# Loading the first pair's keys in one transfer of 18 KB runs instead of two pieces

## The chip, the cores and the metric

The kernel runs on one core of a Trainium2 chip. The metric is device time in microseconds (us), as the median of several runs. A profile is one execution in which every instruction and every DMA packet was recorded; its span runs from the first to the last instruction and is 1.8 us shorter than the time that is reported for the same execution.

DMA packets carry a clock of their own, called the record clock here. It reads about 10.3 us more than the span's clock: the last packet of the fp32 weight strip ends at 14.59 on it, and the cast that waits for that strip starts at 4.29 us.

## The reference

Attention with keys and values averaged over groups of eight rows, followed by a soft mixture of experts with 32 slots. Shortened:

```python
# q, k, v: (8, 8, 576, 64) fp32; phi: (512, 32); w1: (8, 512, 1024); w2: (8, 1024, 512)
k_p = k.reshape(B, H, 72, 8, D).mean(axis=3);  v_p = the same of v
attn = softmax(q @ k_p.T / sqrt(D));  x = (attn @ v_p) laid out as (4608, 512)
logits = x @ phi
slot_input = softmax(logits, axis=0).T @ x                  # 32 slots, 4 per expert
slot_out[e] = relu(slot_input[e] @ w1[e]) @ w2[e]
out = softmax(logits, axis=1) @ slot_out                    # (4608, 512) fp32
```

## The kernel before

The batch is worked in four pairs. For each pair, q, k and v are loaded from fp32 in HBM to bf16 in SBUF by transfers that the Pool engine issues; these share one software queue with nearly all of the expert weights. A load into a buffer that is in use is issued only when its readers have finished. The parts that matter:

```python
big = ctx.enter_context(tc.tile_pool(name="big", bufs=4))       # q, k, v of a pair share four buffers

def load_pair(src, pair, name, cuts=()):
    t = big.tile([128, NT, D], BF, name=name, tag="big")        # NT = 72 rows of 64 per partition
    rows = src[2 * pair:2 * pair + 2].rearrange("b h (i t) d -> (b h i) t d", t=NT)
    for t0, t1 in zip((0,) + cuts, cuts + (NT,)):
        nc.gpsimd.dma_start(out=t[:, t0:t1], in_=rows[:, t0:t1])
    return t

nc.sync.dma_start(out=w1_f, in_=w1_rows[:, 0])                  # fp32 strip on another queue
k_sb[0] = load_pair(k, 0, "k_sb", cuts=(4 * POOL,))             # 32 rows, then 40 rows
q_sb[0] = load_pair(q, 0, "q_sb")
... # identity; cast of w1_f; then phi, v of pair 0, k of pair 1, q of pair 1, ...

def pool_stage(src, dst):                                       # averages groups of eight rows
    for r0 in range(0, NR, 4):                                  # NR = 9 groups: 0-3, 4-7, 8
        ... matmuls of src rows 8*r0 ... against pmat into pool_ps ...
        nc.scalar.copy(out=dst[:, r0:r0 + nr], in_=ps[:, 0:nr])

load_w2(E - 1, xpool, "xs", pieces=2)                           # the last load: two halves of the columns
...
for c in range(2):                                              # the end: per half of the columns
    second(E - 1, c)
    slots_out(c)
    for g in range(3):
        output(g, halves[c])
```

The softmax here doesn't subtract the row's maximum and nothing guards it: scores larger than these inputs give would overflow.

Of the kernel before, what the change touches and what calls it, by code (L numbers as in the profile page):

```python
# [18 lines left out]
def kernel(  # L19
# [10 lines left out]
    nc = tc.nc  # L30

    B, H, S, D = q.shape
    POOL = 8
# [11 lines left out]
    NT = S // NI  # L45
# [18 lines left out]
    pool_order = ctx.enter_context(ExitStack())  # L64
    pool_order.enter_context(tc.manual_schedule(engines={ET.Pool}))

    def load_pair(src, pair, name, cuts=()):
        t = big.tile([128, NT, D], BF, name=name, tag="big")
        rows = src[2 * pair:2 * pair + 2].rearrange("b h (i t) d -> (b h i) t d", t=NT)
        for t0, t1 in zip((0,) + cuts, cuts + (NT,)):  # L70
            nc.gpsimd.dma_start(out=t[:, t0:t1], in_=rows[:, t0:t1])
        return t

    w1_sb = persist.tile([128, E, DJ, F], BF)
# [13 lines left out]
    k_sb, q_sb, v_sb = [None] * NP, [None] * NP, [None] * NP  # L88
# [7 lines left out]

    hT = persist.tile([128, E, FJ, NS], BF)
    nc.vector.memset(hT, 0.0)
    k_sb[0] = load_pair(k, 0, "k_sb", cuts=(4 * POOL,))
    q_sb[0] = load_pair(q, 0, "q_sb")  # L100
    ident = consts.tile([128, 128], BF)
    make_identity(nc, ident)
    nc.gpsimd.tensor_copy(out=w1_sb[:, E - 1, 0], in_=w1_f)
    early.close()
    phi_f = persist.tile([128, DM // 128, NS], FP)
    nc.gpsimd.dma_start(out=phi_f, in_=moe_phi.rearrange("(p j) e -> p j e", j=DM // 128))
    v_sb[0] = load_pair(v, 0, "v_sb")


# [33 lines left out]
    for r in range(2):  # L143
        rows = slice(r * D, (r + 1) * D)
        nc.vector.tensor_copy(out=iphi[rows, :, 0:D],
                              in_=ident[rows, rows].rearrange("p d -> p () d").to_broadcast([D, H, D]))
# [301 lines left out]
    for n in [2] * NSMALL + [4] * ((NO - NSMALL) // 2):  # L448
        row0 = sum(128 * g[1] for g in groups)
        step_ = n // 2  # L450
        rows = lambda r, c0=row0 // 2, s=step_: cT[:, r % 2, c0 + r // 2:c0 + 128 * s:s]
# [88 lines left out]
```

## Time and profile before

| | |
|---|---|
| time | 179.69 us, median of 3 runs, 178.59 to 180.0 |
| span of the profiled execution | 175.9 us |
| software queue | 30.74 MB written, 6144 packets |
| first key product | 10.65 us |
| q of pair 0: first transpose | 17.89 us |
| last weights used by PE, first and second half of the columns | 147.19 and 149.82 us |

From the page of the kernel before, in 40 equal slices of 4.4 us: the clock granted to TensorE, the busy share of the DMA engines (9 is 90% or more) and the rate. Below them, for two DMA queues, packets, MB and share of the 16 engines.

```profile
PEclk9998589999999999999997598589965579999555
DMA  5999999999999999999999999999999999799995
GB/s 162 195 215 222 214 217 216 220 212 218 211 218 217 220 212 215 213 219 216 212 218 216 218 209 216 216 218 218 212 214 220 214 191 131 254 401 417 417 419 237
...
q0 software_dynamic: 6144, 30.74, 85.6%
...
q8 instruction: 11, 0.18, 0.4%
```

The DMA engines are busy without a gap and move about 216 GB/s up to slice 32. The stores take the last slices at about 417 GB/s.

The timeline of the kernel before, for the first pair's keys and q (start, duration, engine, line, operation, count; in brackets the idle time before it and what ended it):

```profile
1.25 1.23 POOL L71 DMA_DIRECT2D k_sb<-in_k_dram  x2 [0.81 <-POOLq L524]
...
10.65 1.06 PE L192 MATMUL pool_ps<-pmat,k_sb 128*128 128x128 bf16 x16
...
12.44 1.29 PE L192 MATMUL pool_ps<-pmat,k_sb 128*128 128x128 bf16 x20 [0.73 <-DMA k_sb<-in_k_dram]
...
14.03 0.53 POOL L71 DMA_DIRECT2D q_sb<-in_q_dram  x1 [7.06 <-PE pool_ps L192]
...
17.89 1.46 PE L207 MATMUL q_ps<-ident,q_sb 128*128 128x128 bf16 x12 [4.16 <-DMA q_sb<-in_q_dram]
```

PE pools the first piece while the second is on its way, then waits more than 4 us for q. The early start buys nothing that the next step can use.

The last part of the timeline of the kernel before: the matmuls of the last expert, for the two halves of the columns, and the first store.

```profile
147.19 0.40 PE L475 MATMUL so_ps_2188<-w_xs,hT 128*32 128x256 bf16 x8 [0.18 <-DMA w_xs<-in_moe_w_dram]
149.21 0.60 SPq L494 DMA_DIRECT2D out_dram<-o_sb_2328  x1
149.82 0.40 PE L475 MATMUL so_ps_2189<-w_xs,hT 128*32 128x256 bf16 x8 [0.28 <-DMA w_xs<-in_moe_w_dram]
```

The chain of waits of the kernel before has this as its longest piece (start, duration):

```profile
118.59 28.55 DMA w_xs<-in_moe_w_dram
```

The last weights are issued at 118.6 us and are waited for until 147.2 us: they sit behind everything else in the queue.

### The profile page before, as it was taken

How to read it: one execution, taken by the hardware profiler on the slowest of the kernel's cores; microseconds unless marked ns; L12 is line 12 of the kernel's file. 1: busy time of each engine (PE TensorE's matmuls, PEld its weight loads, DVE VectorE, ACT ScalarE, POOL GpSimd, SP SyncE). 2: the span in 40 equal slices, each digit the busy share in tenths (PEclk: the TensorE clock that was granted, in tenths of full speed). 3: DMA queues.
4: the chain of work that ended last, by engine and by line, in shares of the span. 5: the costliest groups of instructions: out<-in, count | busy, mean ns of one | idle time of the engine just before them, and what ended most of it. 6: DMA issues, size and time to landing. Idle time of an engine off the chain costs nothing.

```text
span 175.9 us, 3513 instructions
## 1 busy us (share of the span) xinstructions
PE 135.8 (77%) x1467; PEld 85.0 (48%) x1467; DVE 91.6 (52%) x251; ACT 79.3 (45%) x144; POOL 19.1 (11%) x38
## 2 busy tenths in 40 slices
PE   4981789899999999999998995998762277674700
PEld 1450657666876587865775453644651123221200
DVE  6200651378767868878688369643600003784530
ACT  3011158788958669676698540111100001684420
POOL 5501011102110601111001111003000000000000
PEclk9998589999999999999997598589965579999555
DMA  5999999999999999999999999999999999799995
GB/s 162 195 215 222 214 217 216 220 212 218 211 218 217 220 212 215 213 219 216 212 218 216 218 209 216 216 218 218 212 214 220 214 191 131 254 401 417 417 419 237
DMA packets 9086, 40.91 MB, mean 233 GB/s; under 512 B 736, under 2 KB 4320, under 8 KB 4976
## 3 DMA queue, kind: packets, MB, share of 16 engines
q0 software_dynamic: 6144, 30.74, 85.6%
q1 hardware_dynamic: 2928, 9.96, 14.3%
q8 instruction: 11, 0.18, 0.4%
q14 instruction: 3, 0.02, 0.0%
HBM read 61.93 MB, written 9.44 MB: 406 GB/s over the span
## 4 chain that ended last, share of the span: by engine, by line
DMA 43%; PE 36%; DVE 8%; ACT 7%; issue 1%; POOL 1%; DVEq 0%; SPq 0%; ACTq 0%
DMA w_xs<-in_moe_w_dram 16%; DMA q_sb<-in_q_dram 10%; DMA phi_f<-in_moe_phi_dram 7%; PE sc L265 6%; PE pool_ps L192 6%; PE G_ps L296 6%; PE u_ps L278 6%; PE q_ps L207 4%; DMA out_dram<-o_sb_2435 3%; DMA out_dram<-o_sb_2393 3%; DVE xs L284 2%; DMA w_f<-in_moe_w_dram 2%; PE lg_ps L290 2%; DMA out_dram<-o_sb_2336 1%; PE fold_ps L218 1%; ACT ex_1641 L266 1%
## 5 line engine op out<-in xcount | busy, mean ns | idle before, releaser
L284 DVE TENSOR_TENSOR xs<-u_ps,rec 128x384 bf16<-128x384 f32 x72 | 39.4, 552 | 1.6
L265 PE MATMUL sc<-qT,kp 64*72 64x288 bf16 x128 | 23.1, 311 | 0.6 <-ACT ex_1642 L266 0.4
L283 DVE RECIPROCAL rec<-u_ps 128x4 f32<-128x4 f32 x72 | 12.5, 175 | 16.8 <-PE u_ps L278 16.4
L207 PE MATMUL q_ps<-ident,q_sb 128*128 128x128 bf16 x144 | 13.1, 243 | 6.1 <-DMA q_sb<-in_q_dram 4.5
L488 PE MATMUL f_ps<-so,cT 128*128 128x512 bf16 (+1 forms) x42 | 12.0, 390 | 7.0 <-ACT o_sb_2435 L490 1.4
L207 PEld LDWEIGHTS <-q_sb 128*128 128x128 bf16 x144 | 10.0, 109 | 7.9 <-DMA q_sb<-in_q_dram 5.9
L265 PEld LDWEIGHTS <-kp 64*72 64x72 bf16 x128 | 8.7, 108 | 7.8 <-issue 2.0
L296 PE MATMUL G_ps<-xs,ee 128*128 128x512 bf16 x36 | 11.3, 454 | 0.4 <-ACT ee L291 0.4
L490 ACT ACTIVATE o_sb_2328<-f_ps,recR 128x256 f32<-128x256 f32 x1 | 0.5, 473 | 24.5 <-PE f_ps L488 24.5
L211 ACT COPY qT<-q_ps 128x768 bf16<-128x768 bf16 x8 | 6.4, 796 | 11.2 <-PE q_ps L207 11.2
L213 DVE COPY qT<-q_ps 128x768 bf16<-128x768 bf16 x16 | 8.8, 551 | 4.8 <-PE q_ps L207 4.7
L488 PEld LDWEIGHTS <-cT 128*128 128x128 bf16 x42 | 4.3, 103 | 14.2 <-issue 11.8
L195 ACT CAST kpar<-pool_ps 128x512 bf16<-128x512 f32 (+1 forms) x12 | 5.5, 484 | 11.4 <-PE pool_ps L192 11.3
L479 DVE TENSOR_SCALAR so<-so_ps_2188,recC 128x256 bf16<-128x256 f32 x1 | 0.5, 483 | 19.3 <-PE so_ps_2188 L475 19.3
L192 PE MATMUL pool_ps<-pmat,k_sb 128*128 128x128 bf16 x144 | 9.9, 220 | 0.8 <-DMA k_sb<-in_k_dram 0.7
L115 PEld LDWEIGHTS <-zeros 128*128 128x128 bf16 x53 | 5.6, 113 | 10.1 <-issue 4.5
L475 PEld LDWEIGHTS <-hT 128*32 128x32 bf16 x128 | 4.0, 109 | 11.8 <-issue 11.4
L192 PE MATMUL pool_ps<-pmat,v_sb 128*128 128x128 bf16 x144 | 9.6, 220 | 0.0
L192 PEld LDWEIGHTS <-k_sb 128*128 128x128 bf16 x144 | 8.5, 97 | 1.7 <-DMA k_sb<-in_k_dram 0.9
L192 PEld LDWEIGHTS <-v_sb 128*128 128x128 bf16 x144 | 8.2, 98 | 0.7 <-issue 0.2
L238 DVE TENSOR_TENSOR spread<-phi_f,head 128x256 bf16<-128x256 f32 x4 | 1.4, 422 | 12.4 <-DMA phi_f<-in_moe_phi_dram 12.4
L115 PE MATMUL warm_ps<-zeros 128*128 128x512 bf16 x18 | 6.0, 507 | 2.3 <-DVE ones L134 2.3
(171 smaller groups left out, 246.4 us busy)
## 6 DMA issues: line engine op xcount, KB each, us to landing
w_sb<-in_moe_w_dram POOLq DMA_DIRECT2D x7, 1024.0 KB, 31.8
q_sb<-in_q_dram POOLq DMA_DIRECT2D x4, 1152.0 KB, 18.9
v_sb<-in_v_dram POOLq DMA_DIRECT2D x4, 1152.0 KB, 17.1
w_big<-in_moe_w_dram POOLq DMA_DIRECT2D x4, 1024.0 KB, 37.2
k_sb<-in_k_dram POOLq DMA_DIRECT2D x3, 1152.0 KB, 21.6
w_qT<-in_moe_w_dram POOLq DMA_DIRECT2D x2, 1024.0 KB, 36.0
w_xs<-in_moe_w_dram POOLq DMA_DIRECT2D x1, 1024.0 KB, 37.2
w_xs<-in_moe_w_dram POOLq DMA_DIRECT2D x2, 512.0 KB, 29.4
```

What stands on the lines that cost most here:

```text
L115: nc.tensor.matmul(out=ps, lhsT=zeros[:, 0:128], rhs=zeros, start=True, stop=True)
L192: nc.tensor.matmul(out=ps[:, r].rearrange("p n i -> p (n i)"), lhsT=src[:, tt:tt + 2, :].rearrange("p t d -> p (t d)"), rhs=pmat, start=(t ...
L195: nc.scalar.copy(out=dst[:, r0:r0 + nr], in_=ps[:, 0:nr])
L207: nc.tensor.transpose(out=ps[:, t].rearrange("p n i -> p (n i)"), in_=q_sb[pair][:, tt:tt + 2, :].rearrange("p t d -> p (t d)"), identity= ...
L211: nc.scalar.copy(out=dst, in_=ps)
L213: nc.vector.tensor_copy(out=dst, in_=ps)
L265: nc.tensor.matmul(out=ps[:, r, 0:S // 2], lhsT=kp[pair][rows, n], rhs=qT[pair][rows, n], start=True, stop=True)
L278: nc.tensor.matmul(out=ps[rows, hh], lhsT=ex[b][:, hh].rearrange("p r t -> p (r t)")[:, c:c + rows.stop - rows.start], rhs=vp[(2 * pair + ...
L283: nc.vector.reciprocal(out=rec, in_=ps[:, :, XW])
L284: nc.vector.tensor_tensor(out=xs[pair][:, t, qd * HQ:(qd + 1) * HQ, :], in0=ps[:, :, 0:XW], in1=rec.rearrange("p h -> p h ()").to_broadcas ...
L296: nc.tensor.matmul(out=ps, lhsT=ee[:, t].rearrange("p g s -> p (g s)"), rhs=x[:, t, :, 0:D], start=(t == 0), stop=(t == 8))
L488: nc.tensor.matmul(out=f_ps, lhsT=rows(r), rhs=so[:, cols], start=True, stop=True)
```

## The change

The split let PE start on the first 32 rows of keys while the other 40 were still coming. The change drops it: one issue instead of two, and source runs of 18 KB per partition instead of 8 and 10 KB.

```diff
-    def load_pair(src, pair, name, cuts=()):
+    def load_pair(src, pair, name):
         t = big.tile([128, NT, D], BF, name=name, tag="big")
-        rows = src[2 * pair:2 * pair + 2].rearrange("b h (i t) d -> (b h i) t d", t=NT)
-        for t0, t1 in zip((0,) + cuts, cuts + (NT,)):
-            nc.gpsimd.dma_start(out=t[:, t0:t1], in_=rows[:, t0:t1])
+        nc.gpsimd.dma_start(out=t, in_=src[2 * pair:2 * pair + 2].rearrange("b h (i t) d -> (b h i) t d", t=NT))
         return t
 ...
-    k_sb[0] = load_pair(k, 0, "k_sb", cuts=(4 * POOL,))
+    k_sb[0] = load_pair(k, 0, "k_sb")
```

## The prediction

> **What bounds the kernel now.** Until 147 us it is the cast-loading software DMA queue. The forty-slice page shows the DMA engines at 9 tenths in every slice from 4.4 us on; a table of stretches gives a steady 216 GB/s from 24 to 140 us. The chain of waits ends its first part with the last expert weights (issued 118.6 us, landed 147.2 us, 28.6 us of queueing), then come about 23 us of output stores. Loads are issued long before they land: the list of DMA issues has 17 to 22 us for q, k, v and 32 to 37 us for weights. So what happens before 147 us counts only if it changes the queue's start, its work or leaves it empty.
>
> **What the change does.** Pool issues one key transfer (4608 elements per partition) instead of two (2048 and 2560). No instruction moves on PE, DVE, ACT or SP.
>
> 1. *Queue work, a small gain.* The trace's records of single packets give medians of 324 ns for 4096 bytes, 399 for 5120, 625 for 8192 and 700 for 9216. Both pieces cost 723 ns per partition, the whole 700: 23 ns saved. With 128 partitions over 16 engines that is 8 x 23 = 0.18 us, plus one 22 ns completion record: 0.2 us of queue time.
>
> 2. *Issue time, no gain.* Two key issues take 1.23 us on Pool, one about 0.55 to 0.7. The q issue moves from 2.46 to about 1.9 us, but q queues behind the keys anyway, and phi's issue (5.35 us) still waits for the fp32 weight strip, which lands at 4.24 us.
>
> 3. *Pooling starts later, no loss.* Now PE pools the first 16 products from 10.4 to 11.8 us, waits 0.7 us for the second piece and ends near 13.8 us. Afterwards it waits for the whole transfer (landing about 12.2 us), then does 36 products at about 62 ns, ending near 14.6 us. The next work, the q transposes, waits for q until 17.9 us in any case; the fold that reads kpar is at 23.2 us. The refill of the keys' buffer (pair 1's q) goes from 14.0 to about 14.9 us, but v of pair 0 and k of pair 1 (2.3 MB, over 8 us) are queued then, so the queue doesn't run dry.
>
> 4. *Possible side effect.* PE's idle gap before the q transposes shrinks from 4.1 to about 3.2 us. In this trace the clock drops to 0.57 in 18 to 24 us, and those transposes take 120 ns instead of 60. The Trainium skill, "TensorE: Matmul & The Clock Gate", Part 1, says that the clock halves after an idle window of about 3.4 us; the trace agrees so far. The clock may stay up, and pair 0's scores start 1 us sooner. That too is absorbed by the queue.
>
> **On the critical path:** only item 1, 0.2 us of 179.7, about 0.1%. The three runs before spread over 1.4 us.
>
> **Prediction:** 179.5 us, 178.0 to 181.0 us; faster by over 2%: 1%, within 2%: 97%, slower by over 2%: 2%.
>
> **Right if** the page shows 128 fewer software packets; the last weights land at 147.0 +/- 0.5 us; the first key product is at about 12.3 us instead of 10.4; q's first transpose stays at 17.5 to 18 us; DMA stays at 9 in all slices after the first.
> **Wrong if** the first transfer starts or lands much later as one piece (q's transposes then shift by as much, and so does the end), if an idle DMA slice shows a refill that came too late, or if the output stage differs (clock, stores).

## The result, and the profile after

The changed kernel took 179.99 us (179.67 to 180.23, 6 runs) against 179.50 us of the kernel before (178.59 to 180.0, 6 runs). The ratio is 1.0031, with a 95% interval of 1.0005 to 1.0058. A ratio is the mean time of one kernel's runs over that of the other's in the same rounds, so it isn't quite the ratio of the medians.

The interval excludes 1, and the changed kernel's profile is 2.3 us longer than that of the kernel before: 178.2 us against 175.9 us. (The profiled execution of the kernel before took 177.69 us, less than any of its six timed runs.) Taken alone, these two results would say that the one transfer costs something. From the page of the changed kernel:

```profile
PEclk9999657999999999999999975699975569569985
DMA  5999999999999999999999999999999997799995
GB/s 151 165 203 217 221 213 217 217 215 217 215 217 214 217 215 217 216 211 219 217 210 221 213 214 218 213 215 219 215 213 219 210 193 96 239 379 425 425 416 235
...
q0 software_dynamic: 6000, 30.74, 84.7%
```

There are 144 packets fewer: 128 data packets and the 16 four-byte completion records of one transfer. The first slices move less: 151 and 165 GB/s against 162 and 195. The timeline of the changed kernel for the first pair:

```profile
1.25 0.69 POOL L69 DMA_DIRECT2D k_sb<-in_k_dram  x1 [0.80 <-POOLq L522]
...
12.30 2.18 PE L190 MATMUL pool_ps<-pmat,k_sb 128*128 128x128 bf16 x36 [1.88 <-DMA k_sb<-in_k_dram]
...
14.78 0.53 POOL L69 DMA_DIRECT2D q_sb<-in_q_dram  x1 [8.11 <-PE pool_ps L190]
17.80 0.84 PE L205 MATMUL q_ps<-ident,q_sb 128*128 128x128 bf16 x12 [3.32 <-DMA q_sb<-in_q_dram]
```

Pooling now waits for the whole transfer, ends 0.75 us later, and is still idle for 3.3 us before q, which is there at the same time as before (17.80 and 17.89 us). So nothing is lost up to here. Yet the end of the loads has moved. The same part of the timeline of the changed kernel, and the longest piece of its chain of waits:

```profile
149.15 0.40 PE L473 MATMUL so_ps_2187<-w_xs,hT 128*32 128x256 bf16 x8 [0.19 <-DMA w_xs<-in_moe_w_dram]
151.17 0.60 SPq L492 DMA_DIRECT2D out_dram<-o_sb_2327  x1
151.77 0.40 PE L473 MATMUL so_ps_2188<-w_xs,hT 128*32 128x256 bf16 x8 [0.27 <-DMA w_xs<-in_moe_w_dram]
```

```profile
118.28 33.45 DMA w_xs<-in_moe_w_dram
```

The last weights are used 1.95 us later, although q is used 0.1 us sooner. The time was lost somewhere between 18 and 149 us, where the two programs are the same. That is the question for the experiments.

### The profile page after: what moved, and what is told of

Read it like the earlier page. It is cut to its first block, busy times and chain, and to the rows that moved or that the text cites. A ratio compares the mean times of both kernels' runs of the same rounds, so it can differ in the third digit from the quotient of the medians.

```text
span 178.2 us, 3512 instructions
## 1 busy us (share of the span) xinstructions
PE 136.2 (76%) x1467; PEld 85.5 (48%) x1467; DVE 92.0 (52%) x251; ACT 79.5 (45%) x144; POOL 18.4 (10%) x37
## 4 chain that ended last, share of the span: by engine, by line
PE 44%; DMA 33%; ACT 9%; DVE 6%; issue 1%; POOL 1%; DVEq 0%; ACTq 0%; SPq 0%
DMA w_xs<-in_moe_w_dram 19%; PE pool_ps L190 9%; PE sc L263 8%; DMA phi_f<-in_moe_phi_dram 7%; PE u_ps L276 7%; PE q_ps L205 5%; PE G_ps L294 5%; DMA out_dram<-o_sb_2434 3%; DMA out_dram<-o_sb_2392 2%; PE fold_ps L216 2%; DVE xs L282 2%; PE f_ps L486 2%; DMA w_f<-in_moe_w_dram 2%; PE lg_ps L288 2%; ACT ex_1640 L264 1%; ACT ex_1641 L264 1%
## 5 line engine op out<-in xcount | busy, mean ns | idle before, releaser
L486 PE MATMUL f_ps<-so,cT 128*128 128x512 bf16 (+1 forms) x42 | 12.9, 422 | 5.9 <-ACT o_sb_2462 L488 1.4
L205 PE MATMUL q_ps<-ident,q_sb 128*128 128x128 bf16 x144 | 12.6, 234 | 4.7 <-DMA q_sb<-in_q_dram 3.3
L205 PEld LDWEIGHTS <-q_sb 128*128 128x128 bf16 x144 | 9.5, 104 | 6.3 <-DMA q_sb<-in_q_dram 3.5
L190 PE MATMUL pool_ps<-pmat,v_sb 128*128 128x128 bf16 x144 | 10.8, 235 | 0.0
L294 PE MATMUL G_ps<-xs,ee 128*128 128x512 bf16 x36 | 9.8, 407 | 0.4 <-ACT ee L289 0.4
L190 PEld LDWEIGHTS <-v_sb 128*128 128x128 bf16 x144 | 9.5, 107 | 0.8 <-issue 0.2
L193 ACT CAST vpar<-pool_ps 128x512 bf16<-128x512 f32 (+1 forms) x12 | 5.6, 480 | 5.5 <-PE pool_ps L190 5.4
```

The source lines that it names most:

```text
L190: nc.tensor.matmul(out=ps[:, r].rearrange("p n i -> p (n i)"), lhsT=src[:, tt:tt + 2, :].rearrange("p t d -> p (t d)"), rhs=pmat, start=(t ...
L205: nc.tensor.transpose(out=ps[:, t].rearrange("p n i -> p (n i)"), in_=q_sb[pair][:, tt:tt + 2, :].rearrange("p t d -> p (t d)"), identity= ...
L294: nc.tensor.matmul(out=ps, lhsT=ee[:, t].rearrange("p g s -> p (g s)"), rhs=x[:, t, :, 0:D], start=(t == 0), stop=(t == 8))
L486: nc.tensor.matmul(out=f_ps, lhsT=rows(r), rhs=so[:, cols], start=True, stop=True)
```

## The experiments

Six theories were on the table in the end:

- **A**: the large first packets make the queue start slowly. In the first two profiles the slow key packets (those that took over 1.1 times the usual time of their size) were 19 engine-us over that time in sum in the changed kernel, against 8 in the kernel before.
- **B**: chance in the start of the queue.
- **C**: PE pools later, refills a buffer later, or runs on a colder clock, and that costs the time.
- **D**: the number of transfers decides, not the packet size.
- **E**: writing the descriptors of the next loads slows the large packets in flight.
- **F**: the start doesn't differ where it counts; something else on the DMA engines delays the slowest of them.

### The kernel before again, and the changed kernel again

No edit; both are yardsticks.

> The kernel before again, unchanged, as a yardstick for noise. Ratio 1.000 within 0.003 under every theory. The start of the queue: theory A (the whole key transfer starts the queue slowly, and does so every time) expects its packets to look like the first trace of before: 4096 and 5120 byte packets, in sum about 8 engine-us above their usual 324 and 399 ns in the first 20 us, first 2 MB landed some 1 us sooner than in the changed kernel. Theory B (the two traces differ by chance of the start) expects this sum to wander between 8 and 18.

Measured: 178.98 us, ratio 0.9977 (0.9919 to 1.0034); span of its profile 175.8 us.

> The changed kernel again. A: 0.3 to 0.6% slower than before (0.5 to 1.1 us), packets of the keys again slow (sum near 18 engine-us over 700 ns each), last expert weights landing again 1 to 2 us after those of the repeated kernel before. B: ratio 1.000 within 0.002, packets anywhere. C (later pooling, later refill or a cold PE clock costs the time): same ratio as A, but explained by the PE side, so the run with both pieces and late pooling must show it too.

Measured: 179.47 us, ratio 0.9988 (0.9923 to 1.0053). The 0.3% of the first result did not come back, though the interval is too wide to exclude it. The scatter was much larger: both kernels ran from about 177.2 to 180.5 us. The profile is 178.4 us long; this one execution counts as slow by the rule of 1.5% over the kernel's own fastest run. The sum of slow packets was 4.6 engine-us for the kernel before and 18.9 for the changed kernel, so A still stood in the packets, though not in the times.

### Two pieces, but late pooling

```diff
-        for r0 in range(0, NR, 4):
+        for r0 in (8, 4, 0) if late_first else range(0, NR, 4):   # late_first for pair 0's keys
```

> Two pieces as before, but pair 0's pooling takes the second piece's rows first, so PE starts when both have landed, as in the changed kernel (first key product at about 12.3 us instead of 10.4, refill at about 14.9 us). A: ratio 1.000, the queue starts as before. C: ratio 1.003 to 1.006, as in the changed kernel. B: 1.000.

Measured: 178.83 us, ratio 1.0008 (0.9956 to 1.0059). The timeline of this run shows that the edit did what it should: all 36 products in one block at 12.09 us and the refill at 14.57 us, as in the changed kernel.

```profile
12.09 2.18 PE L192 MATMUL pool_ps<-pmat,k_sb 128*128 128x128 bf16 x36 [0.40 <-DMA k_sb<-in_k_dram]
...
14.57 0.53 POOL L71 DMA_DIRECT2D q_sb<-in_q_dram  x1 [7.73 <-PE pool_ps L192]
17.58 0.95 PE L207 MATMUL q_ps<-ident,q_sb 128*128 128x128 bf16 x12 [3.30 <-DMA q_sb<-in_q_dram]
```

Its span is 176.0 us. In this profile the late pooling costs nothing, and the times show no cost either (to within half a per cent), which speaks against C.

### Two pieces, the first one small

```diff
-    k_sb[0] = load_pair(k, 0, "k_sb", cuts=(4 * POOL,))
+    k_sb[0] = load_pair(k, 0, "k_sb", cuts=(POOL,))
```

> Two pieces, cut at 8 rows instead of 32: packets of 1024 and then 8192 bytes. A in the form 'large packets are slow while the queue starts': 8192 byte packets above their 625 ns as in the changed kernel, and most of its loss, ratio 1.003 to 1.005. A in the form 'only the first few packets count, a short first transfer starts faster': ratio 1.000. B and C: 1.000 (C: PE waits 1 us longer than before for its second group, so at most 1.002).

Measured: 179.38 us, ratio 1.0018 (0.9968 to 1.0068), slow packets 13.1 engine-us. It lies between the two kernels and tells nothing apart.

### The changed kernel a third time, halves of the partitions, earlier issues, four pieces

> The changed kernel a third time, for its profile and the yardstick of this chip. Two earlier profiles of it landed 1.2 MB of the software queue's bytes at 21.8 and 22.0 us of the record clock (kernel before and the late-pooling run: 20.2 to 20.7) and ended the queue at 162.1 and 162.4 (before: 159.8 to 160.2). Theory A (the large packets of the first transfer are slow while the queue starts, every time): again 21.5 to 22.2 and 161.5 to 162.6. Timed: between 1.000 and 1.006; the last session's scatter of 3 us hides less than 0.5%.

Measured: 179.28 us, ratio 1.0022 (0.9986 to 1.0059); span 176.7 us. 1.2 MB were in at 20.9 and the queue ended at 160.7, so both expected ranges of A were missed.

Halves of the partitions, whole rows:

```diff
+        if pair == 0 and name == "k_sb":
+            rows = src[0:2].rearrange("b h (i t) d -> (b h i) t d", t=NT)
+            for p0 in (0, 64):
+                nc.gpsimd.dma_start(out=t[p0:p0 + 64], in_=rows[p0:p0 + 64])
+            return t
```

> The keys in two transfers again, but by halves of the partitions: whole rows, 9216 byte packets as in the changed kernel, and two issues as in the kernel before. If packet size makes the slow start (A): 1.2 MB at 21.5 to 22.2, end of the queue 161.5 or later. If the number of transfers or issues does (D): as the kernel before, 20.2 to 20.7 and 159.7 to 160.3.

Measured: 179.55 us, ratio 1.0032 (0.9996 to 1.0069). 1.2 MB were in at 20.6, as D expects, but the queue ended at 160.6, outside D's range.

Earlier issues, in the changed kernel:

```diff
+    nc.gpsimd.dma_start(out=phi_f, ...)          # moved up, from behind the cast of w1_f
+    v_sb[0] = load_pair(v, 0, "v_sb")
+    k_sb[1] = load_pair(k, 1, "k_sb")
     ident = consts.tile([128, 128], BF)
     make_identity(nc, ident)
```

> The changed kernel with phi, v of pair 0 and k of pair 1 issued straight after q (at 2.5 to 4.1 us instead of 5.0 to 6.7). In the two profiles of the changed kernel the slow packets start 5 to 7 us into the span, the same time as those issues. Theory E (writing descriptors for them slows the large packets in flight): the slow packets move to 2.5 to 4.1 us or vanish. A without E: they stay at 5 to 7 us, 1.2 MB again at 21.5 to 22.2.

Measured: 179.53 us, ratio 1.0009 (0.9961 to 1.0058). The slow packets fell to 9.0 engine-us but neither vanished nor moved to 2.5 to 4.1 us (they start from 3.1 to 9.1 us), which speaks against E. 1.2 MB were in at 20.7, and yet the queue ended at 162.3.

Four pieces:

```diff
-    k_sb[0] = load_pair(k, 0, "k_sb", cuts=(4 * POOL,))
+    k_sb[0] = load_pair(k, 0, "k_sb", cuts=(2 * POOL, 4 * POOL, 6 * POOL))
```

> Keys in four pieces (2048, 2048, 2048 and 3072 byte packets), the kernel before taken further. A: no slow start, packets within 10% of their usual time, 1.2 MB at 20.0 to 20.7; the extra packets cost 16 x 24 ns = 0.4 us of queue time against two pieces, so the end of the queue 159.8 to 160.6; ratio 1.000 to 1.003. If the gain goes on with ever smaller pieces: end before 159.6.

Measured: 179.52 us, ratio 1.0035 (1.0003 to 1.0068). The packets of 2048 bytes, whose usual time is 173 ns, were slow too: 16.4 engine-us in sum, almost as much as in the changed kernel. 1.2 MB were in only at 21.5, and the queue ended at 162.0. A had expected otherwise in all three.

After eight runs the measures disagreed with each other: a good start went with a late end, and packets of 2 KB were as slow as packets of 9 KB. The measure was at fault. "1.2 MB landed" is a mean over sixteen DMA engines. The Trainium skill, "DMA: Bandwidth & Descriptors", section "Why a DMA increments its semaphore by 16 and not by 1", says that the engines of a transfer finish independently and that only the full count means that all of the data has landed. The packet records agree: each transfer of this queue ends with 16 four-byte completion records, and the first and the last of them lie 1.4 to 4.9 us apart (from pair 0's v on). What PE waits for is the last of the sixteen.

### Following the slowest engine

So the sixteen completion records of each transfer were sorted, and the last was kept. For the kernel before, the intervals between these last completions repeat the same few numbers (worked out from the packet records). They start at the landing of pair 0's q, taken here together with phi, the 64 KB transfer behind it, which lands at most about 0.2 us later:

```
kernel before        5.47 5.47 5.47 5.47 5.47 5.47 5.47 4.87 5.47 5.47 5.47 4.87 (6x) 3.66 4.87 (6x) 4.66 2.66 2.87
changed kernel       5.47 6.40 5.47 5.47 5.47 5.47 5.47 4.87 5.47 5.47 5.47 4.87 (4x) 5.05 4.87 3.66 4.87 5.79 4.87 (4x) 3.75 2.76 3.66
```

A pair's load takes 5.47 us on an engine, an expert's weights take 4.87 us. The changed kernel has three intervals that are longer, by 0.93, 0.18 and 0.92 us, together 2.03 us. In the record clock, the first runs from 33.7 to 40.1, the second from 108.2 to 113.2 and the third from 126.6 to 132.4; instruction fetches of 16 KB started at 34.9, 110.9 and 127.0. The record of such a fetch is 0.89 to 0.98 us long. The idea is that the engine that serves it falls behind by about that much, and that the landing moves only if this engine is the slowest one or nearly so.

All sixteen completions, followed from one transfer to the next in the same records, show it. (The records do not name the engine; the one completion of sixteen that leaves the common step is taken for one engine.) In the first profile of the kernel before, each of the ten fetches from 34.8 to 138.9 delays one completion, by 0.85 to 1.11 us, and each time one that was 1.3 to 2.9 us ahead of the last, so that the last does not move. In the first profile of the changed kernel, three of the ten fetches delay completions that were only 0.18, 0.93 and 0.19 us ahead of the last, by 1.11, 1.12 and 1.11 us. What is left over, 0.93, 0.19 and 0.92 us, is the three stretches.

All profiles of kernels with an unchanged end, in the record clock; "q landed" includes phi, as above; "lost" is the end of the queue minus this landing minus 131.81 us, which is that difference in the first two profiles of the kernel before:

| kernel | keys landed | q landed | end of the queue | lost after q | span |
|---|---|---|---|---|---|
| before, first profile | 22.76 | 28.39 | 160.19 | 0 | 175.9 |
| before, again | 22.32 | 27.95 | 159.75 | 0 | 175.8 |
| late pooling | 22.17 | 27.80 | 159.92 | 0.31 | 176.0 |
| before, once more (below) | 22.73 | 28.36 | 162.25 | 2.08 | 178.3 |
| changed, first profile | 22.58 | 28.21 | 162.06 | 2.04 | 178.2 |
| changed, again | 22.62 | 28.25 | 162.40 | 2.34 | 178.4 |
| changed, third | 22.22 | 27.85 | 160.67 | 1.01 | 176.7 |
| changed, fourth (below) | 22.46 | 28.09 | 162.15 | 2.25 | 178.2 |
| small first piece | 22.19 | 27.82 | 161.17 | 1.53 | 177.2 |
| halves of the partitions | 21.04 | 26.66 | 160.57 | 2.10 | 176.8 |
| halves, again (below) | 22.31 | 27.96 | 161.74 | 1.97 | 177.7 |
| earlier issues | 22.62 | 28.25 | 162.29 | 2.23 | 178.2 |
| four pieces | 22.34 | 27.97 | 162.04 | 2.26 | 178.5 |

Among the first 24 intervals of these thirteen profiles, 27 are off their usual length by over 0.1 us. In 24 of the 27 a 16 KB fetch started. Fetches fall into 10 of the 24 intervals of any profile, so chance would give about 11 of 27. Two of the other three are one record counted into the neighbouring interval (-0.41 and +0.41). In the third, the 0.32 us of the late-pooling run, a smaller fetch started: 8 KB on queue q14, 0.32 us long. The span follows the end of the queue with an offset of 15.7 to 16.5 us in all thirteen.

The start of the queue does matter in one way. When pair 0's v landed, 1 or 2 engines (the slowest included) were within 1 us of the slowest one in the three profiles that lost least (0 to 0.31 us), and 3 to 10 engines in nine of the ten others (earlier issues: 2). So the more engines start late, the more of them are exposed to a fetch that counts.

This theory, F, was found after the fact, and needed a test on new runs.

### The test of F on new runs

> The kernel before once more. In ten profiles so far the last record of the software queue comes 131.8 us after the slowest DMA engine has finished pair 0's q, plus what that engine lost to 16 KB instruction fetches (0 to 2 of them, each about 0.9 to 1.1 us, seen as a stretched interval between two of its completions where 5.47 or 4.87 us is usual). Theory F (the start is the same, and fetches that hit the slowest engine make the difference): keys' landing at 22.2 to 22.8 of the record clock, end = q's landing + 131.8 + the stretches, to 0.1 us. Theory A (the whole key transfer starts the queue late): this one's keys land sooner than those of the changed kernel in the same call.

Measured: 179.79 us, ratio 0.9968 (0.9933 to 1.0003). This is the kernel before, unchanged, and its profile has a span of 178.3 us, 2.4 us longer than its first. It had lost 2.08 us after q, in stretches of 0.96, 0.14 and 0.97 us, which sum to 2.07; fetches started in all three of these intervals. (That landing plus stretches gives the end is arithmetic; what is tested is where the keys land and whether fetches start in the stretched intervals.) Its slow packets sum to 18.0 engine-us, as many as in the changed kernel. Its end, in the timeline:

```profile
149.37 0.40 PE L475 MATMUL so_ps<-w_xs,hT 128*32 128x256 bf16 x8 [0.18 <-DMA w_xs<-in_moe_w_dram]
...
151.39 1.94 SPq L494 DMA_DIRECT2D out_dram<-o_sb  x3
152.02 0.40 PE L475 MATMUL so_ps<-w_xs,hT 128*32 128x256 bf16 x8 [0.30 <-DMA w_xs<-in_moe_w_dram]
```

Read next to the first profiles, this is the end of the changed kernel (149.15 and 151.77), in a kernel that has the two pieces. Its first slices are as thin as those of the changed kernel too:

```profile
GB/s 153 156 219 224 211 223 209 225 207 221 211 221 211 224 209 219 214 215 215 217 215 215 215 214 218 213 215 219 213 215 217 212 192 82 226 392 423 423 419 235
```

So neither the late end nor the thin start needs the one transfer. A, which ties them to it, falls with this run; that the start varies from one execution to the next, as B has it, stands.

> The changed kernel once more. F: keys' landing on the slowest engine 22.2 to 22.8 as in the kernel before, end = q's landing + 131.8 + the stretches, to 0.1 us; timed ratio 1.000 within 0.004. A: keys and q land 0.5 us or more later than in the repeated kernel before, and the end too, without stretches.

Measured: 179.45 us, ratio 0.9962 (0.9928 to 0.9996), which leans the other way than the first result. Keys and q landed at 22.46 and 28.09, within F's range and not 0.5 us later than in the run above. It lost 2.25 us: 0.53, 0.59 and 0.53 us in intervals with fetches, and 0.58 us in the last three transfers, which were not followed engine by engine. With the fetches' stretches alone, F's "to 0.1 us" is missed by this 0.58 us.

> The keys by halves of the partitions once more. Its one profile landed the keys at 21.0 and q at 26.7, some 1.4 us before every other kernel, and lost 2.1 us of it again to two stretched intervals. If that start is a property of this form: 20.7 to 21.4 and 26.3 to 27.0 again, and with F the time is about 1 us below the changed kernel's in the mean (ratio near 0.995 to 1.000 against before). If it was chance: 22.2 to 22.8.

Measured: 179.74 us, ratio 0.9966 (0.9931 to 1.0001). The keys landed at 22.31 this time. The early landing in its first profile was chance, and there is no better version here.

### Joining the two pieces at the other end of the queue

The same kind of edit, made to the kernel before where nothing is queued behind it:

```diff
-                load_w2(E - 1, xpool, "xs", pieces=2)
+                load_w2(E - 1, xpool, "xs")
```

> The kernel before with the last expert's weights in one transfer instead of two halves of the columns: the same kind of joining, but with nothing queued behind. The two halves take 2.66 us each on an engine, the whole 4.87, so the queue ends about 0.5 us sooner, but the first column half can't start 2.6 us before the end any more: first store issued about 2 us later relative to the slowest engine's start (149.2 in the first profile of before, plus its stretches), the stores end 1 to 2 us later, ratio 1.004 to 1.012. If splitting is as idle there as at the head: 1.000 or below.

Measured: 181.96 us, ratio 1.0094 (1.0059 to 1.0128), so slower by 1.7 us, by an amount outside the scatter of the key experiments (the unchanged kernel came out at 0.9968 in the same set of runs). The queue itself ended 0.4 us sooner after q, once its stretches (1.50 us) are taken off: 132.87 - 1.50 = 131.37 against 131.81. But the matmuls of both column halves now wait for the end of the queue:

```profile
150.89 0.40 PE L475 MATMUL so_ps<-w_xs,hT 128*32 128x256 bf16 x8 [2.41 <-DMA w_xs<-in_moe_w_dram]
...
153.12 20.01 SPq L494 DMA_DIRECT2D out_dram<-o_sb  x14
```

The first store is issued at 153.12 us, 3.9 us later than in the first profile of the kernel before and 1.7 us later than in its last one. The split pays here, where something is waiting for the first piece.

## Why the prediction was right or wrong

**The time: right.** 179.99 us against 179.5 us predicted, inside 178.0 to 181.0. The range of 3 us is about as wide as the scatter and would have held with or without the 0.2 us of item 1. Over four sets of runs the ratio of the changed kernel was 1.0031, 0.9988, 1.0022 and 0.9962. The first and last of these exclude 1 in opposite directions, and in the last set the unchanged kernel itself came out at 0.9968, so the change has no effect that these runs can show, to within about 0.4%.

**Item 1, 0.2 us of queue time saved: mis-sized.** It added up packet durations, 324 + 399 ns against 700 ns. Packets of one engine overlap. In the late-pooling profile one engine that lags behind the others starts its 4096-byte packets every 0.30 us and its 5120-byte packets every 0.38 us, which makes 0.68 us together; a 9216-byte packet costs 5.47 / 8 = 0.684 us. The two pieces cost the engine the same as the whole, to the 0.01 us that can be read there. The mean landing of the keys agrees: 22.50 in the four profiles with the original two pieces and 22.47 in the four of the changed kernel, each with a scatter of about 0.3 us. Starts, not durations, were what a busy engine cost here.

**Item 2, no gain from the saved issue: right.** The one issue takes 0.69 us instead of 1.23 us and q is issued at 1.93 us, but q's first transpose moves only from 17.89 to 17.80 us.

**Item 3, pooling later at no loss: right.** The first product came at 12.30 us (12.3 predicted), the refill at 14.78 us (14.9 predicted). The late-pooling run separates this from the transfer and shows no cost.

**Item 4, the clock: half right.** The first twelve transposes of q ran at the full rate, 0.84 us instead of 1.46 us. The next 24 took 2.89 us in both kernels, and in the changed kernel's first profile the low clock then lasted longer. The stretch from 24 to 34 us, first of the kernel before and then of the changed kernel (duration; busy time of PE, PEld, DVE, ACT, POOL; then the granted clock, the DMA share and GB/s):

```profile
24.00:34.00 10.00, 9.19 (x122) 6.94 (x121) 2.83 (x10) 8.43 (x19) 1.06 (x2) 1.00 1.03 216
```

```profile
24.00:34.00 10.00, 9.52 (x98) 7.13 (x98) 2.57 (x8) 6.39 (x14) 0.53 (x1) 0.74 1.03 215
```

Pair 0's work fell behind instead of gaining 1 us. The DMA rate didn't notice, 216 and 215 GB/s, and the slowest engine's intervals there stayed at 5.47 us except for the fetch: it was absorbed by the queue, as predicted. Part 1 of the Trainium skill's "TensorE: Matmul & The Clock Gate" names an idle window of about 3.4 us. The gap here was 3.3 us, and the granted clock fell to half at 19.0 us, 1.2 us after it. In the kernel before it fell at 16.4 us, 2.7 us into the gap, and in the first profile of the halves at 15.9 us, 2.4 us into a gap of 2.97 us. So the clock fell there before 3.4 us without a product had passed, and the length of the gap does not tell when it falls.

**"The last weights land at 147.0 +/- 0.5 us": wrong.** They were used at 149.15 us. The step that failed is "what happens before 147 us counts only if it changes the queue's start, its work or leaves it empty". It treats the queue as one stream of 216 GB/s. It is sixteen, the slowest decides, and these engines also carry other queues. In the changed kernel's first profile three instruction fetches hit an engine at or near the slowest and cost 0.93, 0.18 and 0.92 us, together 2.03 us; to be explained were 2.05 us (the last weights used 1.96 us later, although q came 0.09 us sooner). Over all profiles 0 to 3 fetches counted, by 0.1 to 1.1 us each, in the kernel before as in the changed one. The mark of 147.2 us was luck of the first profile: none of its fetches hit an engine less than 1.3 us ahead of the slowest. The condition "DMA stays at 9 in all slices after the first" is not met to the letter by either page, which has a 7 where the loads end.

**Open.** Timed executions have no packet records, so that their scatter of 3 us has this cause too is inferred from the span following the end of the queue in thirteen profiles; it isn't shown run by run. Why the changed kernel's six first runs lay within 0.6 us of each other at the upper end is open as well, as is why some engines start the queue 2 to 3 us behind the others. The fast engines were later on average in the changed kernel (1.2 MB in at 21.6 against 20.7), but the two ranges overlap (20.9 to 22.0 and 20.2 to 21.6). The landings of the first transfers don't depend on them, but the exposure to fetches does: 7, 5, 3 and 10 engines within 1 us of the slowest in the changed kernel's four profiles, 2, 1, 1 and 5 in the four with the original pieces. Whether the one transfer makes such a start more likely can't be settled by four profiles each; the timed ratios leave room for no more than about 0.4%.

## What to carry to other kernels

Joining the pieces of a transfer at the head of a long queue was worth nothing here, where the next step waits for a later transfer anyway; at the tail, where compute waits for the first piece, it cost 0.9%. When a queue is the limit, follow the slowest engine's completions, not the mean rate, and compare starts, not durations. Before explaining a difference of 1 to 2% between two profiles, profile the unchanged kernel again: here it reproduced the whole difference by itself.

## What the Trainium skill lacked or had wrong

- "Runtime: NRT & Kernel Launch", "Instruction fetch mechanics", says that instructions come in 16 KiB blocks over a DMA queue and calls the cost of a block "one DMA tail-bump, mostly hidden". The runs agree on the size: 11 fetches of 16,384 bytes per execution. They show a cost that the page lacks: the record of a fetch is 0.89 to 0.98 us long, it delayed the software queue on one of the sixteen engines by 0.85 to 1.44 us in the first two profiles, and the fetches that hit an engine at or near the slowest moved the end of a queue of about 150 us by 0 to 2.3 us.
- "DMA: Bandwidth & Descriptors", "Queues, rings and completion order", says that each engine takes the queue rows in turn, packet by packet. That fits the delays above. The page calls two of the engines usually slower but gives no figure for the spread: in this queue the first and last of the 16 completions of one transfer lay 1.4 to 4.9 us apart.
- The same page's "Rules for kernel authors" advises at least 1 MiB per DMA. Here 0.5 and 0.63 MB in place of 1.13 MB cost an engine the same, 0.68 us per partition, in a queue that had more work behind them. The rule does not say for which state of a queue it holds.
